# One change in an attention and feed-forward kernel: another weight decode, weight pieces as single transfers, outputs issued from ScalarE's queue

## The chip, the cores and the metric

The kernel runs on one core of one Trainium2 chip. A core has TensorE (PE, matrix products), VectorE (DVE), ScalarE (ACT), GpSimd (POOL) and SyncE (SP, which here only issues DMA transfers); each engine takes its own list of instructions strictly in order and waits on semaphores for the others. The metric is the device time of one execution in microseconds (us), lower is better. Times of single instructions come from one profiled execution.

## The reference

Sliding-window attention followed by a feed-forward layer, both over 4 batches of 768 tokens:

```python
# q, k, v: [4, 8, 768, 64] float32; n_global = 8, n_local = 96
rel = pos[:, None] - pos[None, :]
is_global = pos[None, :] < n_global
is_local = (rel >= 0) & (rel < n_local)
dist = where(is_global & ~is_local, n_local, abs(rel))
scores = q @ k.T / 8 - slopes[h] * dist          # slopes[h] = 2 ** -(h + 1)
scores = where(is_global | is_local, scores, -1e9)
a = exp(scores - max(scores)); a = a / (sum(a) + 1e-9)
x = (a @ v), heads side by side                  # [3072, 512]
h = x @ w_in                                     # w_in [512, 2048]
g = 0.5 * h * (1 + erf(h / sqrt(2)))
return g @ w_out                                 # w_out [2048, 512]
```

w_in and w_out arrive as float64, 16 MB together. The chip gets them as 64-bit words and has to make float32 of them itself.

## The kernel before

**Products.** Every float32 operand of a large product is kept as a high part in TensorE's fast 32-bit format (fp32r) and a low part, which is the remainder; one product is then three matmuls (high by high, low by high, high by low). `hi_pool` (L145) makes a high part on POOL, `lo_dve` (L148) a remainder on DVE.

**Steps.** The 3,072 tokens are 12 chunks of 256, and the 2,048 columns of the hidden layer are 8 slices of 256. A step T is one chunk with one slice, 96 in all. In a step, `m1` (L468) makes the hidden values h with 24 matmuls; `gelu` applies GELU on ACT (tile gr, L478), takes the high part gh on POOL (L145) and the remainder gl on DVE (L148); `m2` (L495) adds the step to the chunk's result acc with 12 matmuls. At a chunk's last slice ACT copies acc into a tile o (L501), and o goes out by a DMA that SP issues (L502). Attention of a later chunk is woven between (scores s L339 and L343, minimum mn L348 on DVE, exponential L363 on ACT, transposes t L389, probabilities pt L392 and L396, products av L417 and L431). Chunks 0 and 1 (`NATIVE`) do their attention in plain float32 at the start, scaled by xs L422 and turned by xt, xh, xl L452, L454.

**Weights.** The weights are used by all chunks, so they are decoded once, slice by slice at the steps given by `DECODE` (steps −4 to 2, before and around the first products). A slice is four pieces of 128 partitions by 512 words: two of w_in, two of w_out, 32 pieces in all. `load_words` (DMA at L159, issued by SP) brings a piece into a raw buffer, 8 bytes a word as two int32 halves, lw (low) and hw (high); the raw buffers are five of pool `ws`, and four of `stg` for the last slice. A w_in piece is two runs of 2 KB per partition, a w_out piece one of 4 KB. `split_weights` then makes float32 from a piece:

- ACT L184: the rounding bits, lw scaled by 2^-29, as an integer, into lw's place
- DVE L186: high word masked and shifted left by 3, into a tile wb (pool `sm`, tag o, two buffers)
- POOL L188: wb plus the rounding bits, an integer add
- DVE L189: sign and top bit of hw (and) joined with wb (or), into hw's place; this is the weight as float32
- ACT L198: high part winh or wouth (for pieces 12 and 26 POOL does it, `HI_POOL`)
- DVE L200: the remainder winl or woutl (for piece 7 POOL does it, `LO_POOL`)

The decode is right for words within a range of exponents. `check_words` (L209 to L211, three ACT passes on a second load of each piece, at steps 17 to 48, with a scratch tile cq) finds whether one is outside; then a slow general path runs behind the fast one. It does not run with these inputs.

**Order.** A scheduler that simulates the engines sets the order of each engine's list from the program's order and its own costs; waits are placed by data dependence, and by buffers that must come free.

Of the kernel before, what the change touches and what calls it, by code (L numbers as in the profile page):

```python
# [65 lines left out]
class Fast:  # L66
    def __init__(self, tc, ctx, qT, kT, v, w_in, w_out, out, limits):
        self.tc, self.nc = tc, tc.nc
        self.qT, self.kT, self.v, self.w_in, self.w_out, self.out = qT, kT, v, w_in, w_out, out
# [80 lines left out]
    def word_src(self, s, i):  # L150
        if i < 2:
            return self.w_in[i * 256:(i + 1) * 256, s * 512:(s + 1) * 512].rearrange("(d p) f -> p d f", p=P)
        r = s * 256 + (i - 2) * P
        return self.w_out[r:r + P, :].rearrange("p (d f) -> p d f", d=2)

    def load_words(self, s, i, use):
        pool, tag = (self.ws, "ws") if use == "w" and s < NST - 1 else (self.stg, "stage")
        w = pool.tile([P, 2, 256, 2], I32, name=f"{use}{s}_{i}", tag=tag)
        ins = self.nc.sync.dma_start(w.rearrange("p d f t -> p d (f t)"), self.word_src(s, i)).ins  # L159
# [10 lines left out]
    def split_weights(self, s):  # L170
# [9 lines left out]
        for i in range(4):  # L180
            w = self.raw.pop((s, i, "w"))
            lw, hw = w[:, :, :, 0], w[:, :, :, 1]
            a, t = hw, lw
            nc.scalar.activation(out=t, in_=lw.bitcast(U32), func=AF.Copy, scale=2.0 ** -29)  # L184
            bt = self.sm.tile([P, 2, 256], I32, name=f"wb{s}_{i}", tag="o")
            nc.vector.tensor_scalar(out=bt, in0=hw, scalar1=0x07FFFFFF, scalar2=3,  # L186
                                    op0=ALU.bitwise_and, op1=ALU.logical_shift_left)
            nc.gpsimd.tensor_tensor(out=bt, in0=bt, in1=t, op=ALU.add)  # L188
            nc.vector.scalar_tensor_tensor(out=a, in0=hw, scalar=-0x40000000, in1=bt,  # L189
                                           op0=ALU.bitwise_and, op1=ALU.bitwise_or)  # L190
            if i < 2:
                hi, lo = (x[:, 2 * i:2 * i + 2, :] for x in self.win[s])
            else:
                hi, lo = (x[:, i - 2, :].rearrange("p (d f) -> p d f", d=2) for x in self.wout[s])
            if s * 4 + i in HI_POOL:
                self.hi_pool(hi, a.bitcast(F32))
            else:
                nc.scalar.copy(hi, a.bitcast(F32))  # L198
            eng = nc.gpsimd if s * 4 + i in LO_POOL else nc.vector
            eng.tensor_tensor(out=lo, in0=a.bitcast(F32), in1=hi.bitcast(F32), op=ALU.subtract)  # L200
# [282 lines left out]
    def m2(self, t, k):  # L483
# [14 lines left out]
        if s == NST - 1:  # L498
            o = self.sm.tile([P, DM], F32, name=f"o{c}_{k}", tag="o")
            r = c * CT + k * P  # L500
            nc.scalar.copy(o, acc)  # L501
            nc.sync.dma_start(self.out[r:r + P, :], o)  # L502
# [99 lines left out]
def round_words(nc, pool, out, src):  # L602
    n = out.shape[1]
# [3 lines left out]
    nc.sync.dma_start(w.rearrange("p f t -> p (f t)"), src)  # L607
# [31 lines left out]
def general(tc, qT, kT, v, w_in, w_out, out, limits):  # L639
# [131 lines left out]
```

## Time and profile before

| | before |
|---|---|
| time, median of 3 runs | 737.29 us (737.2 to 737.31) |
| span of the profiled execution, the only time of its own that the page gives | 735.9 us |
| TensorE (PE) busy | 709.4 us (96%) |
| VectorE (DVE) busy | 481.6 us (65%) |
| ScalarE (ACT) busy | 420.9 us (57%) |
| GpSimd (POOL) busy | 349.4 us (47%) |
| chain of work that ended last | PE 85%, DVE 8%, DMA 2% |

Busy shares are averages over a span whose parts differ, so the table is read with the one by stretches of time in the prediction: the weights are loaded and decoded in the first 126 us, and from there on the steps run alike. The runs' time is 1.4 us longer than the span of the profiled execution. In the rows below, out<-in gives the tiles, "wb<-wb,w" for example the tile wb made from wb and w; "x32 | 31.3, 978" is the count, the busy time in us and the mean in ns; what stands behind the second bar is idle time of that engine just before, and who ended it.

### The profile page before, as it was taken

Reading aid. Unit: us, or ns where it says so; the run is one execution under the profiler, and the core shown is the slowest. Engines: PE = TensorE matmul, PEld = TensorE weight load, DVE = VectorE, ACT = ScalarE, POOL = GpSimd, SP = SyncE. Lnnn points to the kernel's source line nnn. Section 1 sums busy time; section 2 is a strip of 40 time slices with the busy share of each in tenths; the row PEclk is TensorE's granted clock in tenths of the full one; section 3 lists DMA queues with packets and bytes.
Section 4 is the critical chain, followed back from the end, with each engine's and each line's share of the span. In section 5 each row is a group of like instructions: output and inputs, shape, how many; then the busy total and the mean of one; then the engine's idle time right before and its main releaser. Section 6 shows DMA issues by size and latency. Waiting matters only on the chain.

```text
span 735.9 us, 13621 instructions
## 1 busy us (share of the span) xinstructions
PE 709.4 (96%) x4617; PEld 642.8 (87%) x4617; DVE 481.6 (65%) x1219; ACT 420.9 (57%) x1032; POOL 349.4 (47%) x607
## 2 busy tenths in 40 slices
PE   6899878999999999999999999999999999999996
PEld 4778667899999999999999999999999999999995
DVE  6989999757846856746756757757657758643111
ACT  5658544555759769769669556355355455452101
POOL 4666666674445555543444545543444545431110
PEclk9999999999999999999999999999999999999999
DMA  8964563333526546535546513223213211100000
GB/s 264 263 191 143 175 213 81 117 83 101 146 78 171 166 123 177 158 108 158 160 125 174 153 44 87 72 62 94 76 47 109 83 29 44 45 15 1 29 1 33
DMA packets 78492, 80.92 MB, mean 110 GB/s; under 512 B 12368, under 2 KB 63056, under 8 KB 78416
## 3 DMA queue, kind: packets, MB, share of 16 engines
q1 hardware_dynamic: 78416, 79.98, 37.5%
q8 instruction: 38, 0.62, 0.4%
q14 instruction: 38, 0.31, 0.1%
HBM read 73.66 MB, written 6.29 MB: 109 GB/s over the span
## 4 chain that ended last, share of the span: by engine, by line
PE 85%; DVE 8%; DMA 2%; issue 1%; ACT 1%; SPq 1%; POOL 1%; POOLq 0%; DVEq 0%; ACTq 0%
PE h L468 35%; PE acc L495 33%; PE t L389 5%; PE s L343 5%; PE av L431 5%; DMA w<-w_in 2%; DVE winl L200 2%; DVE w L189 2%; PE s L339 2%; DVE woutl L200 1%; DVE wb L186 1%; PE av L417 1%; DVE gl L148 1%; ACT n L363 0%; DVE n L348 0%
## 5 line engine op out<-in xcount | busy, mean ns | idle before, releaser
L468 PE MATMUL h<-xh,winh 128*128 128x256 f32 x768 | 221.1, 289 | 1.5 <-ACT xh L454 1.4
L468 PE MATMUL h<-xh,winl 128*128 128x256 f32 x768 | 218.6, 285 | 0.4 <-DVE winl L200 0.4
L468 PE MATMUL h<-xl,winh 128*128 128x256 f32 x768 | 218.9, 285 | 0.0
L495 PE MATMUL acc<-wouth,gl 128*128 128x512 f32 x384 | 150.0, 399 | 7.2 <-DVE gl L148 7.2
L495 PE MATMUL acc<-wouth,gh 128*128 128x512 f32 x384 | 154.4, 402 | 0.9 <-POOL gh L145 0.9
L468 PEld LDWEIGHTS h<-xh,winh 128*128 128x128 f32 x768 | 146.9, 192 | 7.2 <-ACT xh L454 1.8
L495 PE MATMUL acc<-woutl,gh 128*128 128x512 f32 x384 | 152.4, 397 | 0.0
L468 PEld LDWEIGHTS h<-xl,winh 128*128 128x128 f32 x768 | 147.2, 192 | 3.7 <-issue 0.3
L148 DVE TENSOR_TENSOR gl<-gr,gh 128x512 fp32r<-128x512 f32 x96 | 68.2, 710 | 122.9 <-POOL gh L145 122.3
L468 PEld LDWEIGHTS h<-xh,winl 128*128 128x128 f32 x768 | 147.3, 192 | 0.8 <-DVE winl L200 0.6
L478 ACT ACTIVATE gr<-h 128x512 f32<-128x512 f32 x96 | 57.3, 597 | 82.9 <-PE h L468 75.0
L376 POOL TENSOR_SCALAR n<-n,su 128x256 f32<-128x256 f32 (+1 forms) x160 | 71.2, 466 | 55.2 <-DVE su L368 37.5
L145 POOL TENSOR_SCALAR gh<-gr 128x512 fp32r<-128x512 f32 x96 | 64.0, 667 | 69.6 <-ACT gr L478 69.6
L363 ACT ACTIVATE n<-n,mn 128x256 f32<-128x256 f32 (+1 forms) x192 | 91.8, 480 | 8.3 <-DVE mn L348 8.0
L145 POOL TENSOR_SCALAR vt<-vr 128x256 fp32r<-128x256 f32 (+1 forms) x80 | 34.1, 426 | 130.8 <-PE av L431 83.6
L495 PEld LDWEIGHTS acc<-wouth,gl 128*128 128x128 f32 x384 | 72.8, 190 | 24.4 <-DVE gl L148 9.0
L495 PEld LDWEIGHTS acc<-wouth,gh 128*128 128x128 f32 x384 | 73.2, 191 | 12.3 <-POOL gh L145 1.3
L495 PEld LDWEIGHTS acc<-woutl,gh 128*128 128x128 f32 x384 | 73.2, 190 | 11.8
L348 DVE CUSTOM_DVE_ANT_0 n<-s,pen 128x256 f32<-128x256 f32 (+1 forms) x192 | 69.3, 394 | 16.1 <-PE s L343 13.6
L396 ACT CAST pt<-t 128x512 fp32r<-128x512 f32 (+1 forms) x80 | 44.3, 553 | 60.6 <-PE t L389 56.2
L438 ACT COPY t<-av 64x256 f32<-64x256 f32 x80 | 29.3, 367 | 83.0 <-PE av L431 79.9
L188 POOL TENSOR_TENSOR wb<-wb,w 128x512 int32<-128x512 int32 x32 | 48.0, 1501 | 36.6 <-DVE wb L186 17.3
(92 smaller groups left out, 1158.2 us busy)
## 6 DMA issues: line engine op xcount, KB each, us to landing
kr<-kT SPq DMA_DIRECT2D x112, 112.0 KB, 2.8
qr<-qT SPq DMA_DIRECT2D x88, 128.0 KB, 2.9
w<-w_in SPq DMA_DIRECT2D x16, 512.0 KB, 4.7
w<-w_out SPq DMA_DIRECT2D x16, 512.0 KB, 4.5
c<-w_in SPq DMA_DIRECT2D x16, 512.0 KB, 4.2
c<-w_out SPq DMA_DIRECT2D x16, 512.0 KB, 4.4
vr<-v SPq DMA_DIRECT2D x48, 128.0 KB, 2.3
out<-o SPq DMA_DIRECT2D x24, 256.0 KB, 2.1
```

Of the source, the lines that this page charges most:

```text
L145: self.nc.gpsimd.tensor_scalar(out=out, in0=in_, scalar1=scale, scalar2=0.0, op0=ALU.mult, op1=ALU.add)
L148: self.nc.vector.tensor_tensor(out=out, in0=in_, in1=hi.bitcast(F32), op=ALU.subtract)
L188: nc.gpsimd.tensor_tensor(out=bt, in0=bt, in1=t, op=ALU.add)
L343: nc.tensor.matmul(sp[:, j, :w], lhsT=qq[:, hh, j * P:(j + 1) * P], rhs=kt[:, t, 0 if first else j, :w], start=t == 0, stop=t == 1)
L348: nc.vector.tensor_tensor_reduce(out=nn[:, j, :w], in0=sp[:, j, :w], in1=pen, scale=-slope(h), scalar=3e38, op0=ALU.add, op1=ALU.min, accu ...
L363: ins = nc.scalar.activation(out=nn[:, j, :w], in_=nn[:, j, :w], func=AF.Exp, bias=mn[:, i:i + 1], scale=-1.0, accum_out=su[:, i:i + 1])
L376: nc.gpsimd.tensor_scalar(out=nn[:, j, :w], in0=nn[:, j, :w], scalar1=su[:, i:i + 1], scalar2=0.0, op0=ALU.mult, op1=ALU.add)
L389: nc.tensor.transpose(tp[:, i, :], nn[:, j, a * P:(a + 1) * P], self.ident)
L396: nc.scalar.copy(pt[:, :, 0, :], tp[:, :n, :])
L468: nc.tensor.matmul(hp[:, f, :], lhsT=w[:, d, f * P:(f + 1) * P], rhs=x[:, d, :], start=n == 0, stop=n == 3 * NP - 1)
L478: self.table(nc.scalar.activation(out=gr, in_=hp, func=AF.Gelu))
L495: nc.tensor.matmul(acc, lhsT=g[:, f, ks], rhs=w[:, f, :], start=s == 0 and n == 0, stop=s == NST - 1 and n == 5)
```

## The change

The host lays both weight arrays out as one array `w` of 32 pieces, each [128, 512] words, so that any piece is one run of 4 KB per partition. The decode becomes:

- ACT L181: the rounding bits as before, but written as a 16-bit integer into the low half of lw
- ACT L182, new: the sign of the high word (−1, 0 or 1) as bfloat16 into the upper half of lw
- DVE L184: high word shifted left by 3, without a mask, into wb
- DVE L185: wb plus lw as an integer add. The sign and rounding bits come in with the one add. The instruction list shows it as a custom instruction (ISA) on 1,024 half-words
- ACT L191: high part, 2 times wb, for all 32 pieces
- DVE L192: the remainder, 2 times wb minus the high part, for all 32 pieces

POOL has no part in the decode any more. The raw buffer is last read by the add; wb is held until the remainder is made. The check works in place on the raw words, with other constants, without the scratch tile. The output DMAs are issued by ACT (L495) behind its copy of acc (L494) instead of by SP.

```diff
-# work that GpSimd takes over from the other engines: weight halves (high, low part), V of a chunk
-HI_POOL, LO_POOL, V_POOL = (12, 26), (7,), (2,)
+V_POOL = (2,)
...
     def load_words(self, s, i, use):
         pool, tag = (self.ws, "ws") if use == "w" and s < NST - 1 else (self.stg, "stage")
-        w = pool.tile([P, 2, 256, 2], I32, name=f"{use}{s}_{i}", tag=tag)
-        ins = self.nc.sync.dma_start(w.rearrange("p d f t -> p d (f t)"), self.word_src(s, i)).ins
+        w = pool.tile([P, 512, 2], I32, name=f"{use}{s}_{i}", tag=tag)
+        ins = self.nc.sync.dma_start(w.rearrange("p f t -> p (f t)"), self.w[s * 4 + i]).ins
...
             w = self.raw.pop((s, i, "w"))
-            lw, hw = w[:, :, :, 0], w[:, :, :, 1]
-            a, t = hw, lw
-            nc.scalar.activation(out=t, in_=lw.bitcast(U32), func=AF.Copy, scale=2.0 ** -29)
-            bt = self.sm.tile([P, 2, 256], I32, name=f"wb{s}_{i}", tag="o")
-            nc.vector.tensor_scalar(out=bt, in0=hw, scalar1=0x07FFFFFF, scalar2=3,
-                                    op0=ALU.bitwise_and, op1=ALU.logical_shift_left)
-            nc.gpsimd.tensor_tensor(out=bt, in0=bt, in1=t, op=ALU.add)
-            nc.vector.scalar_tensor_tensor(out=a, in0=hw, scalar=-0x40000000, in1=bt,
-                                           op0=ALU.bitwise_and, op1=ALU.bitwise_or)
+            lw, hw = w[:, :, 0], w[:, :, 1]
+            half = w.bitcast(U16)
+            nc.scalar.activation(out=half[:, :, 0], in_=lw.bitcast(U32), func=AF.Copy, scale=2.0 ** -29)
+            nc.scalar.activation(out=half[:, :, 1].bitcast(BF16), in_=hw, func=AF.Sign)
+            a = self.sm.tile([P, 512], I32, name=f"wb{s}_{i}", tag="o")
+            nc.vector.tensor_scalar(out=a, in0=hw, scalar1=3, scalar2=None, op0=ALU.logical_shift_left)
+            nc.vector.tensor_tensor(out=a, in0=a, in1=lw, op=ALU.add)
+            af = a.bitcast(F32)
...
-            if s * 4 + i in HI_POOL:
-                self.hi_pool(hi, a.bitcast(F32))
-            else:
-                nc.scalar.copy(hi, a.bitcast(F32))
-            eng = nc.gpsimd if s * 4 + i in LO_POOL else nc.vector
-            eng.tensor_tensor(out=lo, in0=a.bitcast(F32), in1=hi.bitcast(F32), op=ALU.subtract)
+            nc.scalar.activation(out=hi, in_=af, func=AF.Copy, scale=2.0)
+            nc.vector.scalar_tensor_tensor(out=lo, in0=af, scalar=2.0, in1=hi.bitcast(F32),
+                                           op0=ALU.mult, op1=ALU.subtract)
...
-        q = self.stg.tile([P, 2, 256], F32, name=f"cq{n}", tag="stage", padded_shape=[P, 4, 256])
-        nc.scalar.activation(out=q, in_=w[:, :, :, 1], func=AF.Square, scale=2.0 ** -27)
+        q = w[:, :, 1].bitcast(F32)
+        nc.scalar.activation(out=q, in_=w[:, :, 1], func=AF.Square, scale=2.0 ** -27, bias=self.cbias[:, 2:3])
...
             nc.scalar.copy(o, acc)
-            nc.sync.dma_start(self.out[r:r + P, :], o)
+            nc.scalar.dma_start(self.out[r:r + P, :], o)
```

**How the order changes.** In the names below, w4_1 is the raw buffer of slice 4, piece 1, wb4_1 its scratch tile, winh4 and winl4 (wouth4, woutl4) the parts of slice 4; the last number only tells tiles of the program apart. First DVE's list before, around the decode of slice 4:

```order
L148 TENSOR_TENSOR gl1_873<-gr1_874,gh1_872 128x512
L186 TENSOR_SCALAR wb4_2_827<-w4_2_245 128x512
L189 SCALAR_TENSOR_TENSOR w4_1_243<-w4_1_243,wb4_1_820 128x512
L200 TENSOR_TENSOR winl4_809<-w4_0_241,winh4_808 128x512
L186 TENSOR_SCALAR wb4_3_834<-w4_3_247 128x512
L200 TENSOR_TENSOR winl4_809<-w4_1_243,winh4_808 128x512
L189 SCALAR_TENSOR_TENSOR w4_2_245<-w4_2_245,wb4_2_827 128x512
L148 TENSOR_TENSOR xl1_603<-xt1_2_897,xh1_602 128x256
L422 TENSOR_TENSOR xs1_3_913<-av1_3_892,su1_3_665 128x2x2x64
L186 TENSOR_SCALAR wb5_0_972<-w5_0_249 128x512
```

and after, at the same place:

```order
L149 TENSOR_TENSOR gl0_781<-gr0_782,gh0_780 128x512
L184 TENSOR_SCALAR wb4_1_822<-w4_1_244 128x512
L185 ISA wb4_1_822<-w4_1_244,wb4_1_822 128x1024
L192 SCALAR_TENSOR_TENSOR winl4_810<-wb4_0_815,winh4_809 128x512
L184 TENSOR_SCALAR wb4_2_829<-w4_2_246 128x512
L149 TENSOR_TENSOR gl1_874<-gr1_875,gh1_873 128x512
L185 ISA wb4_2_829<-w4_2_246,wb4_2_829 128x1024
L192 SCALAR_TENSOR_TENSOR winl4_810<-wb4_1_822,winh4_809 128x512
L415 TENSOR_TENSOR xs1_2_807<-av1_2_793,su1_2_589 128x2x2x64
L149 TENSOR_TENSOR xl1_604<-xt1_1_798,xh1_603 128x256
```

The place of the and/or (L189) is taken by the add (L185, the ISA row), which stands right behind its own shift (L184) or one instruction after it; before, the POOL add lay between them. The remainder (L192) reads wb and no longer the raw buffer.

ACT's list before, at that place:

```order
L478 ACTIVATE gr1_874<-h1_840 128x512
L184 ACTIVATE w4_1_243<-w4_1_243 128x512
L198 CAST wouth3_717<-w3_3_239 128x512
L184 ACTIVATE w4_2_245<-w4_2_245 128x512
L392 COPY pt1_7_883<-t1_7_878 128x512
L198 CAST winh4_808<-w4_0_241 128x512
L184 ACTIVATE w4_3_247<-w4_3_247 128x512
L198 CAST winh4_808<-w4_1_243 128x512
L478 ACTIVATE gr2_942<-h2_915 128x512
```

and after:

```order
L182 ACTIVATE w4_2_246<-w4_2_246 128x512
L181 ACTIVATE w4_3_248<-w4_3_248 128x512
L385 COPY pt1_5_791<-t1_5_786 128x512
L181 ACTIVATE w5_0_250<-w5_0_250 128x512
L191 ACTIVATE winh4_809<-wb4_0_815 128x512
L471 ACTIVATE gr1_875<-h1_841 128x512
L182 ACTIVATE w4_3_248<-w4_3_248 128x512
L181 ACTIVATE w5_1_252<-w5_1_252 128x512
L191 ACTIVATE winh4_809<-wb4_1_822 128x512
L182 ACTIVATE w5_0_250<-w5_0_250 128x512
```

Three passes per piece stand there (L181, L182, L191) where two stood (L184, L198), and the two that prepare a piece are up to a GELU (L471) apart, because the scheduler puts other work between.

POOL's integer adds (L188) are gone from its list; the high parts gh of GELU stay there (L145 before, L146 after). At the end of the first chunk the outputs stood on SP between loads of the next chunks:

```order
L246 DMA kr3_2_1855<-kT 64x2x256 x2
L502 DMA out<-o0_0_1428 128x512
L252 DMA qr3_0_1573<-qT 64x2x256
L502 DMA out<-o0_1_1470 128x512
L252 DMA qr3_0_1573<-qT 64x2x256
L296 DMA vr2_2_1584<-v 128x2x128
L297 DMA vr2_2_1584<-v 96x2x128
```

and after they stand on ACT, right behind their copies:

```order
L471 ACTIVATE gr8_1419<-h8_1392 128x512
L494 COPY o0_0_1429<-acc0_0_886 128x512
L495 DMA out<-o0_0_1429 128x512
L494 COPY o0_1_1471<-acc0_1_903 128x512
L495 DMA out<-o0_1_1471 128x512
L389 CAST pt2_0_1492<-t2_0_1487 128x4x128
```

Both outputs have moved to ACT's list, ahead of the probabilities pt that follow there; the loads on SP have closed up. PE's list keeps its products in almost the same order, and ACT has as many table loads as before.

More of the change, by code (lines that the diff above doesn't have):

```diff
@@ L12 @@
 U32 = mybir.dt.uint32
+U16 = mybir.dt.uint16
 AF = mybir.ActivationFunctionType
@@ L66, with __init__ @@
 class Fast:
-    def __init__(self, tc, ctx, qT, kT, v, w_in, w_out, out, limits):
+    def __init__(self, tc, ctx, qT, kT, v, w, out, limits):
         self.tc, self.nc = tc, tc.nc
-        self.qT, self.kT, self.v, self.w_in, self.w_out, self.out = qT, kT, v, w_in, w_out, out
+        self.qT, self.kT, self.v, self.w, self.out = qT, kT, v, w, out
         self.limits = limits
@@ L112, in consts @@
         self.wbad = const.tile([P, 32], F32, name="wbad")
-        self.cbias = const.tile([P, 2], F32, name="cbias")
-        nc.vector.memset(self.cbias[:, 0:1], -65.0)
-        nc.vector.memset(self.cbias[:, 1:2], -240.0)
+        self.cbias = const.tile([P, 3], F32, name="cbias")
+        for i, x in enumerate((-64.25, -63.0, 0.5)):
+            nc.vector.memset(self.cbias[:, i:i + 1], x)
         ta = self.stg.tile([P, 4, 256], F32, name="ta", tag="stage")
@@ L602, in round_words @@
 def round_words(nc, pool, out, src):
-    n = out.shape[1]
+    n = 512
     ti = lambda name: pool.tile([P, n], I32, name=name)
@@ L606, in round_words @@
     w = pool.tile([P, n, 2], I32, name="r_w")
-    nc.sync.dma_start(w.rearrange("p f t -> p (f t)"), src)
+    for k, x in enumerate(src):
+        m = n // len(src)
+        nc.sync.dma_start(w[:, k * m:(k + 1) * m, :].rearrange("p f t -> p (f t)"), x)
     lw, hw = w[:, :, 0], w[:, :, 1]
@@ L636, in round_words, with general @@
     nc.vector.tensor_copy(out, m)
-def general(tc, qT, kT, v, w_in, w_out, out, limits):
+def general(tc, qT, kT, v, w, out, limits):
     nc = tc.nc
@@ L654, in general @@
                 for f in range(NP):
+                    cols = slice(d % 2 * 512, d % 2 * 512 + 512)
                     round_words(nc, rw, wi[:, d, f * 512:(f + 1) * 512],
-                                w_in[d * P:(d + 1) * P, f * 1024:(f + 1) * 1024])
+                                [w[(2 * f + k) * 4 + d // 2, :, cols] for k in range(2)])
             for f in range(NF):
-                round_words(nc, rw, wo[:, f, :], w_out[f * P:(f + 1) * P, :])
+                round_words(nc, rw, wo[:, f, :], [w[f // 2 * 4 + 2 + f % 2]])
         icol = cst.tile([P, S], I32, name="g_icol")
@@ L734, in general, with body @@
                 nc.sync.dma_start(out[bass.ds(b * S + i * P, P), :], o)
-def body(tc, qT, kT, v, w_in, w_out, limits, out):
+def body(tc, qT, kT, v, w, limits, out):
     nc = tc.nc
-    w_in, w_out = w_in.bitcast(I32), w_out.bitcast(I32)
+    w = w.bitcast(I32)
     with tc.tile_pool(name="flagp", bufs=1) as fp:
@@ L742, in body @@
         with ExitStack() as ctx:
-            fast = Fast(tc, ctx, qT, kT, v, w_in, w_out, out, limits)
+            fast = Fast(tc, ctx, qT, kT, v, w, out, limits)
             fast.run()
@@ L747, in body @@
         with tc.If(fv):
-            general(tc, qT, kT, v, w_in, w_out, out, limits)
+            general(tc, qT, kT, v, w, out, limits)
 def kernel(q, k, v, n_global, n_local, moe_w_in, moe_w_out):
@@ L760 @@
         "v": np.ascontiguousarray(v.transpose(0, 2, 1, 3)).reshape(B, S, DM),
-        "w_in": np.ascontiguousarray(moe_w_in).view(np.int64),
-        "w_out": np.ascontiguousarray(moe_w_out).view(np.int64),
+        "w": np.ascontiguousarray(w),
         "limits": np.array([n_local, n_global]),
```

12 lines of the change are left out of this document (5 added, 7 removed).

## The prediction

> **What bounds the kernel now.** I read three views in this order: a table of busy time by stretch of the span, the list of what TensorE (PE) waits for, and the groups of VectorE (DVE), GpSimd (POOL) and ScalarE (ACT) work in the one stretch where PE has holes. The columns of the first are PE, weight load, DVE, ACT and POOL busy time, each with its count, then the clock that PE was granted, the DMA share and the traffic.
>
> ```profile
> core 0: us, PE busy (x) PEld busy (x) DVE busy (x) ACT busy (x) POOL busy (x), PEclk, DMA share, GB/s
> 12.00:37.00 25.00, 21.83 (x83) 17.95 (x84) 22.68 (x53) 17.10 (x45) 16.31 (x14) 1.00 0.97 288
> 37.00:60.00 23.00, 23.00 (x106) 18.19 (x106) 20.52 (x53) 14.54 (x40) 15.48 (x17) 1.00 0.59 173
> 60.00:126.00 66.00, 54.55 (x333) 46.78 (x332) 65.71 (x100) 34.79 (x67) 40.48 (x33) 0.95 0.50 156
> 126.00:200.00 74.00, 73.52 (x506) 67.79 (x505) 54.03 (x151) 44.50 (x113) 43.98 (x86) 1.00 0.38 108
> 200.00:400.00 200.00, 200.00 (x1361) 184.86 (x1360) 130.35 (x353) 155.57 (x377) 95.64 (x186) 1.00 0.52 147
> ```
>
> From 126 us on PE is full (73.52 of 74, then 200 of 200), and the change leaves its matmuls alone: whatever happens to another engine there is worth nothing unless it makes PE wait. From 60 to 126 PE has 66.00 − 54.55 = 11.45 us of holes while DVE is busy 65.71 of 66.00: DVE bounds this stretch. From 12 to 37 there are 3.17 us of holes under a DMA share of 0.97, and from 37 to 60 there are none. So 14.6 us is the most that filling holes behind 12 us can bring.
>
> Who is waited for in the stretch from 60 to 126, and the only wait after it:
>
> ```profile
> PE acc L495 <- DVE gl L148: 7.2, 5, 2.3
> PE xt L452 <- DVE xs L422: 2.0, 1, 2.0
> ...
> PE s L343 <- DVE k L148: 0.4, 1, 0.4
> ```
>
> The reader is to see that the decode itself is hardly waited for. It is the GELU remainder gl that comes late, since it stands in the DVE's line behind decode work.
>
> **VectorE's side of the change.** The DVE and POOL groups of the same stretch (busy us, mean ns of one):
>
> ```profile
> L189 DVE SCALAR_TENSOR_TENSOR w<-w,wb 128x512 int32<-128x512 int32 x20 | 19.8, 990 | 0.0
> L200 DVE TENSOR_TENSOR winl<-w,winh 128x512 fp32r<-128x512 f32 x10 | 14.5, 1452 | 0.0
> L200 DVE TENSOR_TENSOR woutl<-w,wouth 128x512 fp32r<-128x512 f32 x12 | 14.2, 1181 | 0.1
> L186 DVE TENSOR_SCALAR wb<-w 128x512 int32<-128x512 int32 x19 | 10.4, 550 | 0.1
> L188 POOL TENSOR_TENSOR wb<-wb,w 128x512 int32<-128x512 int32 x20 | 30.9, 1547 | 21.2 <-DVE wb L186 16.1 <-ACT winh L198 2.0 <-ACT xh L454 1.7
> ```
>
> and a few of them one by one (start, duration):
>
> ```profile
> 84.89 0.68 DVE L189 SCALAR_TENSOR_TENSOR w<-w,wb 128x512 int32<-128x512 int32 x1
> ...
> 88.15 0.68 DVE L200 TENSOR_TENSOR woutl<-w,wouth 128x512 fp32r<-128x512 f32 x1
> 88.75 1.79 DVE L189 SCALAR_TENSOR_TENSOR w<-w,wb 128x512 int32<-128x512 int32 x1
> 90.80 0.41 DVE L186 TENSOR_SCALAR wb<-w 128x512 int32<-128x512 int32 x1
> ...
> 93.47 0.84 DVE L186 TENSOR_SCALAR wb<-w 128x512 int32<-128x512 int32 x1
> ...
> 88.46 1.53 POOL L188 TENSOR_TENSOR wb<-wb,w 128x512 int32<-128x512 int32 x1 [1.72 <-ACT xh L454]
> 92.97 1.06 POOL L145 TENSOR_SCALAR gh<-gr 128x512 fp32r<-128x512 f32 x1
> ```
>
> The same DVE instruction takes 0.68 us alone and 1.79 us when POOL's integer add L188 (88.46 to 89.99) lies over it: 1.11 us of its life is the POOL add's. So the means are inflated, and the excess over 0.68 is what the adds cost DVE: L189 20 × (0.990 − 0.682) = 6.2, winl 10 × (1.452 − 0.682) = 7.7, woutl 12 × (1.181 − 0.682) = 6.0, together 19.9 us. I leave out L186's excess, 19 × 0.14 = 2.7, since the row at 93.47 shows it beside POOL's gh, which stays. Taking L188 off POOL gives −19.9 us of DVE time in this stretch (at most −22.6).
>
> The and/or L189 goes and one integer add comes in its place. In the changed kernel's instruction order it is a custom instruction on 1,024 half-words, and the trace has no 16-bit DVE instruction. From below it is bounded by L189 itself, 0.68: same words, two inputs, one of them every second word. From above by a custom instruction that handles one element per step:
>
> ```profile
> L348 DVE CUSTOM_DVE_ANT_0 n<-s,pen 128x256 f32<-128x256 f32 x24 | 9.3, 415 | 1.3 <-PE s L339 1.3
> L348 DVE CUSTOM_DVE_ANT_0 n<-s,pen 128x128 f32<-128x128 f32 x4 | 1.1, 269 | 0.0
> ```
>
> 128 more elements cost 146 ns, so 1,024 would take 0.415 + 768 × 0.00114 = 1.29 us. I take 0.80, near L189, because the bytes per partition are L189's and L348 shows no surcharge for being custom (the plain 0.41 us of a 256-element row). That is +0.12 × 20 = +2.4 us (0 to +12.2). The shift loses its mask and stays at 0.41. The remainder becomes a three-operand form of the same 512 elements; L189 and L200 are such a pair, both 0.68, so nothing. One remainder comes back from POOL, +0.6, put here at worst. Net on DVE between 60 and 126: −19.9 + 2.4 + 0.6 = −17 us, 65.7 to about 49, which is less than PE's 54.55. DVE stops being the bound; PE or ACT is next.
>
> **ScalarE's side.** All 32 pieces get one more ACT pass (the sign), and the two high halves that POOL made come to ACT. Nearest rows, first one by one, then the groups from 12 to 126 us with the idle time before them:
>
> ```profile
> 15.87 0.70 ACT L184 ACTIVATE w<-w 128x512 int32<-128x512 uint32 x1
> 16.44 0.67 ACT L198 CAST winh<-w 128x512 fp32r<-128x512 f32 x1
> L184 ACT ACTIVATE w<-w 128x512 int32<-128x512 uint32 x32 | 21.9, 686 | 12.5 <-DMA w<-w_in 6.9 <-DMA w<-w_out 5.6
> L198 ACT CAST wouth<-w 128x512 fp32r<-128x512 f32 x15 | 10.0, 668 | 11.4 <-DVE w L189 11.3
> ```
>
> Starts are 0.57 apart, so a pass occupies ACT for 0.57 (0.70 if nothing overlaps). From 60 to 126 that is 20 × 0.57 + 2 × 0.57 = +12.5 us: 34.8 becomes 47. ACT is the engine to watch. The most that it is busy over a long stretch in this trace is 155.57 of 200 (0.78); at 0.78 its 47 us need 60 us, at PE's floor of 54.55 it would have to be busy 0.87 of the time. Its old idle time was partly waiting for the very DVE instructions that shrink (L198 for L189, 11.3 us). I take the middle of the two, 57 us for the stretch of 66: −9. From 12 to 37 the loads are at 0.97, so of the 3.17 us there I take 1, for POOL being freer. ACT's table loads stay the same in number.
>
> **Loads, outputs, checks.** A piece as one contiguous run:
>
> ```profile
> w<-w_in SPq DMA_DIRECT2D x16, 512.0 KB, 4.7
> w<-w_out SPq DMA_DIRECT2D x16, 512.0 KB, 4.5
> SPq L159 <- DVE winl L200: 17.0, 6, 4.3
> SPq L502 <- ACT o L501: 112.2, 17, 39.7
> L502 SPq DMA_DIRECT2D out<-o x24: 337/368/867, 134.3 to 730.5; - x24
> ```
>
> w_out pieces already have that form, so 0.2 us of latency for each of 16 pieces, hidden because loads wait for free buffers (17.0 us for winl alone); if that cover went, 3 us. The raw buffer now comes free after the add, two instructions earlier, which can only help; the wb buffer (two of them) is instead held until the remainder is done, but the next shift stands behind that remainder on the same engine anyway: 0. The outputs leave SP, where loads stood 112.2 us behind them, yet PE lost 0.4 us after 126: nothing to gain. On ACT's queue they cost 24 × 0.37 = 9 us over 600, behind which GELU and exponentials stand; ACT is at 0.78 at worst (200 to 400) and PE never waits for it there: 0, and 9 us if ACT were full. At the end it shows:
>
> ```profile
> 729.64 1.60 SPq L502 DMA_DIRECT2D out<-o  x2
> 729.93 0.58 ACT L501 COPY o<-acc 128x512 f32<-128x512 f32 x1 [0.32 <-PE acc L495]
> ```
>
> The last copy must now wait for the first output's issue on its own engine; with 0.37 to 0.87 from 729.64 it starts 0.1 to 0.6 late: +0.3. The check keeps its three ACT passes and loses a scratch tile: 0, hidden like the outputs.
>
> **Sum.** −9 − 1 + 0.3 = −9.7. The profiled execution has a span of 735.9 us; the runs give 737.2 to 737.31, median 737.29, so 1.4 us lies around the span, and I keep it. 735.9 − 9.7 + 1.4 = 727.6 us, 722 to 732 for this case: 722 with all 14.6 us of holes gone, 732 with ACT at 0.78 and the add dearer than taken. A measurement of this kernel can tell about 0.2% (1.5 us) from no change.
>
> **Rivals.**
> (a) The add goes at one half-word per step, 1.29 us. DVE between 60 and 126 is then 65.7 − 19.9 + 12.2 + 0.6 = 58.6, above PE's and level with ACT's need; two engines in order that feed each other do not both run full, so I give 62 of 66: about 733. For it speaks that one operand is every second word; against it that L189 reads so too, at 0.68. The Trainium skill (VectorE: DVE Perf Modes, "Mode 2×_1P — pack two bf16 into one 32-bit read") says that two 16-bit elements a cycle need a 16-bit type and step ±1, which adjacent halves within a word meet and every second word does not: by that rule this rival holds, 733 in place of 727.6. No row here has a 16-bit instruction that could test it.
>
> (b) Slower. ACT takes DVE's place: rounding, sign and high half of every piece, GELU and the PSUM copies now stand in one fixed line, DVE's add waits for the sign, its remainder for the high half, and gl behind them. The 47 us of ACT fill 66 at a busy share of 0.71; below that the stretch gets longer. From 12 to 37 ACT is at 17.10 of 25 (0.68), which would give 69, +3; at 0.64 it is 73, +7. I price it at +5: 742. Against it: it waited then for loads (12.5 us) and for DVE (11.3), not for itself.
>
> (c) The clock comes too. Two rows inside the stretch:
>
> ```profile
> 80.00:90.00 10.00, 7.69 (x40) 6.24 (x39) 10.00 (x13) 4.56 (x9) 6.39 (x5) 0.83 0.56 183
> 100.00:110.00 10.00, 6.96 (x36) 5.83 (x35) 9.96 (x12) 6.08 (x12) 6.56 (x6) 0.83 0.73 261
> ```
>
> PE got 0.83 of its clock there, 2 × 10 × 0.17 = 3.4 us lost. With denser work PE's floor falls from 54.55 to 51.2, and if ACT follows to 53 the stretch gives −13, with −1 before it: 723, 720 at best. The Trainium skill (TensorE: Matmul & The Clock Gate, "Part 1: The HAM clock gate") says that the clock halves after an idle window of about 3.4 us; the longest wait listed here is 2.3 us, so the trace shows the loss but not plainly that cause.
>
> (d) No change: the stretch is paced by something else than DVE's length, the loads, say. Against it: the DMA share is 0.50 at 156 GB/s, where 12 to 37 moved 288. About 737.
>
> **Chances.** Main case 0.54, (a) 0.16, (b) 0.09, (c) 0.15, (d) 0.06. (b) is the slower side, 0.09; (d) is same, 0.06; the rest faster, 0.85. The range leaves out (b), (d) and the far end of (c): 719 to 735. The time is that of the main case.
>
> **What would show it.** L189 and L188 gone; the remainder at 0.68 with no 1.79 rows; the add's duration between 0.68 and 1.29 (near 0.80); DVE busy about 49 us of work where 65.7 stood, ACT about 47; PE's wait for gl well under 7.2 us; PE full from about 116 us on instead of 126. Wrong if ACT shows as what PE or DVE waits for with the stretch as long as before, if the sign takes much more than 0.70 us, or if holes open in PE after the stretch, around the outputs on ACT.

## The result, and the profile after

The changed kernel takes 797.15 us (median of 4, 794.09 to 799.18) against 737.25 before, a ratio of 1.081 (1.078 to 1.084): 60 us slower, where 727.6 was forecast. The rival for a slower outcome said 742. All runs named below are compared with runs of the kernel before on the same chip. Two executions in which PE was slow throughout are left out of the times, e8 (1,375 us, of which only durations of single instructions are read) and one of the twelve of e18 (1,115 us).

The table by stretch of the profiled execution after (columns as in the prediction's first table; its span is 793.7 us):

```profile
12.00:37.00 25.00, 16.10 (x57) 12.07 (x57) 14.43 (x45) 23.75 (x44) 3.22 (x5) 1.00 1.00 284
37.00:60.00 23.00, 21.94 (x74) 16.88 (x73) 18.35 (x48) 23.00 (x36) 7.14 (x12) 1.00 0.70 197
60.00:126.00 66.00, 55.02 (x316) 48.64 (x316) 38.29 (x89) 61.49 (x93) 5.10 (x8) 0.92 0.41 132
126.00:200.00 74.00, 68.32 (x440) 61.79 (x438) 47.19 (x116) 41.93 (x94) 34.03 (x63) 0.96 0.33 93
200.00:400.00 200.00, 179.15 (x1158) 157.82 (x1157) 117.48 (x314) 138.80 (x328) 80.95 (x161) 1.00 0.45 128
400.00:700.00 300.00, 293.90 (x1991) 269.69 (x1991) 190.97 (x519) 161.77 (x414) 140.99 (x277) 1.00 0.28 80
```

Two things are new. Up to 126 us ACT is the full engine (23.75 of 25, 23.00 of 23, 61.49 of 66), with DVE down from 65.71 to 38.29; PE starts fewer matmuls from 12 to 126 us (57 + 74 + 316 against 83 + 106 + 333). And from 200 to 400, where PE had been full, it has 20.85 us of holes, with no engine full. The time was lost in two places, and the second was not in the forecast at all.

ACT's groups of the decode, 60 to 126 us:

```profile
L181 ACT ACTIVATE w<-w 128x512 uint16<-128x512 uint32 x17 | 23.3, 1371 | 2.3 <-DMA w<-w 2.3
L182 ACT ACTIVATE w<-w 128x512 bf16<-128x512 int32 x16 | 21.6, 1351 | 0.2
L191 ACT ACTIVATE winh<-wb 128x512 fp32r<-128x512 f32 x8 | 5.2, 658 | 0.0
```

The high part takes 0.66 us as before; the two passes that write 16-bit halves take 1.37 and 1.35, where the like pass had taken 0.686.

The DVE groups of the same stretch are as the forecast had them, the add included:

```profile
L185 DVE CUSTOM_DVE_ANT_0 wb<-w,wb 128x1024 uint16<-128x1024 uint16 x16 | 11.5, 729 | 0.2
L192 DVE SCALAR_TENSOR_TENSOR winl<-wb,winh 128x512 fp32r<-128x512 f32 x8 | 5.4, 690 | 6.9 <-ACT winh L191 6.8
```

The second place shows in the check's first pass, before and after (all 32, idle time of ACT just before them behind the second bar):

```profile
L209 ACT ACTIVATE cq<-c 128x512 f32<-128x512 int32 x32 | 21.5, 672 | 4.1 <-DVE k L148 2.3 <-DMA c<-w_in 1.6
```

```profile
L202 ACT ACTIVATE c<-c,cbias 128x512 f32<-128x512 int32 x32 | 24.1, 762 | 68.8 <-DMA c<-w 61.9 <-DVE gl L149 6.4 <-issue 0.3
```

and at one place in SP's and ACT's timelines after (the load of c is issued at 252.73, behind the loads of q that SP had in front):

```profile
251.42 1.26 SPq L245 DMA_DIRECT2D qr<-qT  x2
252.73 0.59 SPq L154 DMA_DIRECT2D c<-w  x1
```

```profile
250.18 0.48 ACT L389 CAST pt<-t 128x384 fp32r<-128x384 f32 x1
256.70 0.77 ACT L202 ACTIVATE c<-c,cbias 128x512 f32<-128x512 int32 x1 [6.04 <-DMA c<-w]
259.98 0.60 ACT L471 ACTIVATE gr<-h 128x512 f32<-128x512 f32 x1
```

SP had stood still until 247.19, when the third pass of the check before (L204) gave its buffer free. ACT stands idle for 6.04 us in front of a check that nobody waits for, and behind it in the fixed line stand PSUM copies (L431) and a GELU, on which PE's work hangs. 61.9 us of ACT's time goes that way. What PE itself waits for between 126 and 450 us, where it had waited 0.4 us in all before (the four longest):

```profile
PE av L424 <- DVE pt L149: 9.6, 10, 1.8
PE h L461 <- ACT gr L471: 4.1, 3, 2.1
PE acc L488 <- POOL gh L146: 3.5, 8, 0.7
PE s L336 <- DVE mn L341: 3.5, 2, 1.9
```

The pt of the first row is made from a copy of ACT's (L389), the gh of the third from ACT's GELU. The check loads themselves stand in the chain of work that ended last, with 8% of the span, and PE's share of it is 46% where it was 85%:

```profile
PE 46%; ACT 28%; DMA 11%; DVE 7%; issue 4%; SPq 2%; POOL 1%; ACTq 0%; DVEq 0%; POOLq 0%
PE h L461 20%; PE acc L488 19%; DMA c<-w 8%; ACT n L356 5%; ACT w L181 5%; ACT w L182 4%; PE av L424 3%; PE s L336 2%; PE t L382 2%; ACT c L203 2%; ACT c L204 2%; DMA w<-w 2%; ACT gr L471 2%; ACT L471 2%; ACT c L202 2%
```

### The profile page after: what moved, and what is told of

Read it like the earlier page. It is cut to its first block, busy times and chain, and to the rows that moved or that the text cites. A ratio compares the mean times of both kernels' runs of the same rounds, so it can differ in the third digit from the quotient of the medians.

```text
span 793.7 us, 13516 instructions
## 1 busy us (share of the span) xinstructions
PE 728.9 (92%) x4617; PEld 650.4 (82%) x4617; DVE 456.2 (57%) x1221; ACT 477.8 (60%) x1066; POOL 290.8 (37%) x572
## 4 chain that ended last, share of the span: by engine, by line
PE 46%; ACT 28%; DMA 11%; DVE 7%; issue 4%; SPq 2%; POOL 1%; ACTq 0%; DVEq 0%; POOLq 0%
PE h L461 20%; PE acc L488 19%; DMA c<-w 8%; ACT n L356 5%; ACT w L181 5%; ACT w L182 4%; PE av L424 3%; PE s L336 2%; PE t L382 2%; ACT c L203 2%; ACT c L204 2%; DMA w<-w 2%; ACT gr L471 2%; ACT L471 2%; ACT c L202 2%
## 5 line engine op out<-in xcount | busy, mean ns | idle before, releaser
L461 PE MATMUL h<-xh,winh 128*128 128x256 f32 x768 | 224.6, 293 | 18.1 <-ACT gr L471 9.3
L461 PE MATMUL h<-xl,winh 128*128 128x256 f32 x768 | 221.6, 289 | 0.0
L461 PE MATMUL h<-xh,winl 128*128 128x256 f32 x768 | 220.9, 288 | 0.0
L461 PEld LDWEIGHTS h<-xh,winh 128*128 128x128 f32 x768 | 149.4, 195 | 24.9 <-ACT gr L471 10.4
L461 PEld LDWEIGHTS h<-xl,winh 128*128 128x128 f32 x768 | 150.0, 195 | 4.7 <-issue 0.7
L461 PEld LDWEIGHTS h<-xh,winl 128*128 128x128 f32 x768 | 149.9, 195 | 1.6 <-DVE wb L184 0.7
L149 DVE TENSOR_TENSOR gl<-gr,gh 128x512 fp32r<-128x512 f32 x96 | 71.2, 742 | 127.6 <-POOL gh L146 127.4
L146 POOL TENSOR_SCALAR gh<-gr 128x512 fp32r<-128x512 f32 x96 | 62.0, 645 | 168.3 <-ACT gr L471 168.0
L471 ACT ACTIVATE gr<-h 128x512 f32<-128x512 f32 x96 | 57.7, 601 | 89.3 <-PE h L461 76.7
L146 POOL TENSOR_SCALAR vt<-vr 128x256 fp32r<-128x256 f32 (+1 forms) x80 | 32.6, 407 | 132.7 <-PE av L424 57.8
L389 ACT CAST pt<-t 128x512 fp32r<-128x512 f32 (+1 forms) x80 | 44.3, 555 | 53.4 <-PE t L382 52.0
L432 DVE TENSOR_TENSOR t<-av,t 64x256 f32<-64x256 f32 x80 | 33.6, 420 | 55.9 <-ACT t L431 55.0
L382 PE MATMUL t<-ident,n 128*128 128x128 f32 x352 | 59.4, 290 | 6.8 <-POOL n L369 2.7
```

Source lines behind the costliest of these rows:

```text
L146: self.nc.gpsimd.tensor_scalar(out=out, in0=in_, scalar1=scale, scalar2=0.0, op0=ALU.mult, op1=ALU.add)
L149: self.nc.vector.tensor_tensor(out=out, in0=in_, in1=hi.bitcast(F32), op=ALU.subtract)
L382: nc.tensor.transpose(tp[:, i, :], nn[:, j, a * P:(a + 1) * P], self.ident)
L389: nc.scalar.copy(pt[:, :, 0, :], tp[:, :n, :])
L432: nc.vector.tensor_tensor(out=t1[hr], in0=av[hr, :, 1, :], in1=t1[hr], op=ALU.add)
L461: nc.tensor.matmul(hp[:, f, :], lhsT=w[:, d, f * P:(f + 1) * P], rhs=x[:, d, :], start=n == 0, stop=n == 3 * NP - 1)
```

## The experiments

Edits are against the changed kernel unless another is named.

**Whose part is it?** Four kernels, each with one part undone.

e1_old_check, the scratch tile of the check back:

```diff
-        q = w[:, :, 1].bitcast(F32)
+        q = self.stg.tile([P, 512], F32, name=f"cq{n}", tag="stage", padded_shape=[P, 1024])
```

> The changed kernel with one thing undone: the check's first pass writes a scratch tile again, so a check's raw words are free after one ScalarE pass and not after three. In the changed kernel ScalarE waits 61.9 us for check loads (c <- w), and PE has 31 us of holes between 140 and 450 us. Theory CHECK (the in-place check keeps the staging buffer, so the next load and with it ScalarE's fixed line come late): those waits fall to the 2 us or so of the kernel before, the 40 us lost behind 142 us come back, time 750 to 762. Theory OUTPUTS (the output DMAs' move to ScalarE's queue upsets the order of loads): no change, 792 to 800. Theory LATE START (the decode ends late and everything behind only follows): no change either, 792 to 800, and the waits for check loads stay.

Measured: 753.61 us (753.21 to 754.5), 43.5 us less. From 200 to 400 PE is full again:

```profile
200.00:400.00 200.00, 200.00 (x1365) 184.91 (x1364) 132.90 (x357) 155.38 (x368) 97.32 (x196) 1.00 0.50 144
```

e2_out_sp, the outputs back on SP:

```diff
-            nc.scalar.dma_start(self.out[r:r + P, :], o)
+            nc.sync.dma_start(self.out[r:r + P, :], o)
```

> The changed kernel with one thing undone: the outputs are issued from SP's queue again. Theory OUTPUTS: time falls by about 40 us to 750 to 765 and ScalarE's waits for check loads go. Theory CHECK: within 5 us of the changed kernel, 790 to 802, the waits for check loads (62 us) stay.

Measured: 794.12 us (792.52 to 794.56). ACT's waits for check loads stay (55.2 us), so the outputs' queue is not the cause.

e3_old_decode, the decode of before in the new layout:

> The changed kernel with the decode of before (rounding bits by ScalarE in full words, shift, add on GpSimd, and/or, high and low part; pieces 7, 12 and 26 as before); single transfers, in-place check and outputs on ScalarE's queue stay. Theory DECODE PLUS CHECK (16 us lost in the decode by 142 us, 42 us behind it by the check): 775 to 785. Theory LATE START (all of the loss comes from the decode): 735 to 745. If the check alone is the whole loss: 792 to 800.

Measured: 772.8 us (770.88 to 773.76), 24 us less and a little below the 775 expected, with the check's waits still there (50.4 us). Theory LATE START falls: the check costs its part whenever the decode ends.

e4_wide, whole words instead of halves:

```diff
-            nc.scalar.activation(out=half[:, :, 0], in_=lw.bitcast(U32), func=AF.Copy, scale=2.0 ** -29)
-            nc.scalar.activation(out=half[:, :, 1].bitcast(BF16), in_=hw, func=AF.Sign)
+            nc.scalar.activation(out=lw, in_=lw.bitcast(U32), func=AF.Copy, scale=2.0 ** -29)
+            nc.scalar.activation(out=lw.bitcast(F32), in_=hw, func=AF.Sign)
```

> The changed kernel with the two ScalarE passes of the decode writing whole 32-bit words over the low word (rounding bits as int32, then the sign as float32 over it) in place of 16-bit halves of it; the number of instructions, inputs and functions are the same, but the rounding bits are lost, so the decoded weights are not the reference's. Theory HALF-WORD WRITES (the 1.36 us of L181 and L182, where the like pass took 0.69, come from writing 16-bit elements): both passes 0.56 to 0.70 us, ScalarE busy 45 to 50 us less before 142 us, and the decode stretch ends 15 to 25 us earlier: time 772 to 782 with the check's loss still in it. Theory STRIDED READ OR SIGN (the cost lies in the read or the function): passes stay at 1.3 to 1.4 us, time 792 to 800.

Measured: 769.74 us (767.1 to 772.76), 27.4 us less, a little more than expected. The two passes (min, median and max in ns):

```profile
L181 ACT ACTIVATE w<-w x32: 657/678/706, 13.1 to 106.1; 128x512 int32<-128x512 uint32 x32
L182 ACT ACTIVATE w<-w x32: 655/678/729, 14.0 to 106.8; 128x512 f32<-128x512 int32 x32
```

Neither the function nor the reading of every second word is slow; the 16-bit writing in this form is.

e9_wide_scratch, e1 and e4 together:

> Both causes taken out of the changed kernel at once: whole-word writes in the two ScalarE passes (the rounding bits are lost, so the weights are not the reference's) and the check with its scratch tile. Theory TWO CAUSES (half-word writes 27 us, missing scratch tile 43.5 us, nothing else): 797.2 - 27.4 - 43.5 = 726, between 722 and 731, which is where the forecast put the change. Rival (the two overlap, or the output queue and the single transfers cost something too): 732 to 745.

Measured: 730.9 us (728.95 to 732.82), ratio 0.9906 (0.9874 to 0.9937). With both causes out, the rest of the change takes about 6 us less than the kernel before. The stretch that the forecast worked on:

```profile
60.00:126.00 66.00, 62.02 (x406) 56.64 (x405) 50.43 (x111) 46.34 (x94) 10.45 (x16) 0.94 0.48 153
```

The forecast's terms stand here: DVE 50.43 (about 49 forecast), ACT 46.34 (47), PE's holes 3.98 of 66 where they were 11.45. So the two causes account for the miss, less some 5 us (the single effects add up to 726). In its profile PE is 20.34 of 23 us busy from 37 to 60, at a granted clock of 0.58, where before it was full at 1.00; whether the 5 us lie there, no run tests.

**Why are half-words dear?** e8_forms writes the rounding pass in four ways (the edit shortened to the outputs):

```diff
+            if i == 0:    out=ah[:, 0:512]                        # 16-bit, packed, in the wb tile
+            elif i == 1:  out=ah (f t)->(f t), t=2, [:, :, 0]      # 16-bit, 4 bytes apart, in the wb tile
+            elif i == 2:  out=half[:, :, 0]                        # 16-bit, 8 bytes apart, in lw
+            else:         out=lw                                   # int32, 8 bytes apart, in lw
```

> The changed kernel with the rounding-bit pass written in four ways, one for each piece of a slice: 16-bit side by side into the scratch tile; 16-bit into every second half-word of the scratch tile (4 bytes apart); 16-bit into the low half of lw as in the changed kernel (8 bytes apart); int32 into lw. The first three lose rounding bits for their pieces or leave the raw low word in the add, so the weights are not the reference's; only durations are read. Theory WIDTH (any 16-bit output costs double): 1.36 us three times, 0.68 for int32. Theory PARTIAL WORD (16-bit elements that lie apart cost double, packed ones do not): 0.68, 1.36, 1.36, 0.68. Theory STRIDE (8 bytes apart): 0.68, 0.68, 1.36, 0.68.

```profile
L184 ACT ACTIVATE wb<-w x8: 656/672/707, 12.6 to 142.3; 128x512 uint16<-128x512 uint32 x8
L186 ACT ACTIVATE wb<-w x8: 779/793/848, 14.6 to 144.1; 128x512 uint16<-128x512 uint32 x8
L188 ACT ACTIVATE w<-w x8: 1327/1352/1401, 17.7 to 131.2; 128x512 uint16<-128x512 uint32 x8
L190 ACT ACTIVATE w<-w x8: 637/686/743, 19.4 to 139.1; 128x512 int32<-128x512 uint32 x8
```

A 16-bit write is as fast as a 32-bit one when packed, a little slower at 4 bytes apart, twice as long at 8. But the third form is also the only 16-bit one in place. e26_forms256 (256 elements a pass) tells distance from place: L185 8 bytes apart in another tile, L188 8 bytes apart in place, L191 4 bytes apart in another tile, L194 int32 in place.

> The rounding pass of the changed kernel in two halves of 256 elements, in four ways by piece: 16-bit 8 bytes apart into the scratch tile; 16-bit 8 bytes apart in place in lw; 16-bit 4 bytes apart into the scratch tile; int32 in place. The first and third leave the raw low word in the add, so the weights are not the reference's; only durations are read. From the 512-element rows (0.672 packed, 0.793 at 4 bytes, 1.352 at 8 bytes in place, 0.686 int32 in place) half the length should take about 0.41 for int32. Theory DISTANCE: the first two alike, 0.70 to 0.80 us, the third about 0.47. Theory IN PLACE: only the second at 0.70 to 0.80, the first 0.45 to 0.55.

```profile
L185 ACT ACTIVATE wb<-w x16: 751/816/872, 13.1 to 123.0; 128x256 uint16<-128x256 uint32 x16
L188 ACT ACTIVATE w<-w x16: 752/791/850, 15.8 to 115.2; 128x256 uint16<-128x256 uint32 x16
L191 ACT ACTIVATE wb<-w x16: 462/484/580, 20.8 to 127.9; 128x256 uint16<-128x256 uint32 x16
L194 ACT ACTIVATE w<-w x16: 412/436/525, 19.7 to 120.0; 128x256 int32<-128x256 uint32 x16
```

It is the distance (0.816 and 0.791 alike). The Trainium skill (SBUF — State Buffer, "Door 1: The DMA port swizzle", its note on cachelines) says that a line has 16 bytes, that two hits on a line are enough for full rate, and that bf16 data may therefore be strided by 8 elements for free. By that rule 4 elements (8 bytes) cost nothing. Here ScalarE's output at that distance cost double, 1.352 us as uint16 and 1.351 as bf16 (L182), and int32 at the same distance nothing (0.686), so for these writes the measurement decides against it.

**Why does the check in place cost 43 us?** e11_hold keeps the raw words through all three passes, and the scratch tile too (against e1):

```diff
-        nc.scalar.activation(out=q, in_=q, func=AF.Relu, ...)
+        nc.scalar.activation(out=w[:, :, 1].bitcast(F32), in_=q, func=AF.Relu, ...)
```

> The variant with the scratch tile for the check (753.61 us), but the third pass writes its result into the raw words, so they are held through all three passes as in the changed kernel while the scratch tile is still taken in turn. Theory HOLD (what costs is that the raw words are kept for three passes): the check loads come late again, their lead over the first pass falls from a median of 11.5 us to about 5, time 785 to 800. Theory TURN (what costs is the missing scratch tile, which changes the turn in which the four staging buffers are given out and so the order of loads and check passes): leads stay near 11, time 752 to 760.

Measured: 757.36 us (755.48 to 758.61), the load's lead over the first pass a median of 9.6 us (from the load's issue to the start of the pass; 11.4 in e1, 11.5 before, 5.0 in the changed kernel). Holding the words for three passes is worth at most some 4 us of the 43.5.

e15_dummy takes a scratch tile and lets GpSimd touch it:

```diff
+        nc.gpsimd.memset(self.stg.tile([P, 512], F32, name=f"cq{n}", tag="stage", padded_shape=[P, 1024])[:, 0:1], 0.0)
```

> The changed kernel as it is, check in place, with one thing added: at each check a scratch tile is taken from the four staging buffers and a single column of it is set to zero by GpSimd. It does no work for the result. Theory TURN (the missing scratch tile changes the turn of the staging buffers and so the order of loads and check passes): leads of the check loads back near 11 us, time 752 to 760 as with the real scratch. Theory IN PLACE (three passes over the raw words, with a bias tile, are the cost): 785 to 800.

Measured: 794.23 us (792.62 to 796.43), lead 4.6 us, ACT's wait for check loads 54.7 us. TURN, which e11 had seemed to bear out, is wrong too: giving out one more staging buffer does nothing by itself. So I compared the written orders. In ACT's list the first pass of check n stands behind GELU n+12 or n+13 in the changed kernel and in e15, and behind n+15 to n+17 in e1 and e11: three to four steps later. That the place moves with the scratch tile of the pass is shown (e1 changes nothing else); the reason is my reading: a pass that needs a scratch buffer has to wait for one in the scheduler's reckoning as well. e23_pin adds one rule of order and nothing else:

```diff
-        nc.scalar.activation(out=q, in_=w[:, :, 1], func=AF.Square, ...)
+        first = nc.scalar.activation(out=q, in_=w[:, :, 1], func=AF.Square, ...)
+        self.after(first.ins, self.last_gelu, "check behind its step")
...
+        self.last_gelu = g.ins
```

> The changed kernel as it is, check in place and no scratch tile, with one order added: the first pass of check n must stand behind GELU n+17 in ScalarE's list (it stood behind n+12 or n+13; with the scratch tile behind n+15 to n+17). Theory PLACE (the pass stands in ScalarE's fixed line about four steps ahead of where it did, so the line waits for a load that SP could not issue earlier): leads near 11 us, ScalarE's waits for check loads under 10 us, time 750 to 760. Theory IN PLACE (the passes themselves, or the staging buffers they hold, are the cost): 785 to 800.

Measured: 758.11 us (755.44 to 760.17), the lead a median of 16.6 us. ACT's wait for check loads is gone, and nothing else of the check in place was undone. The first pass as it then stands:

```profile
L202 ACT ACTIVATE c<-c,cbias x32: 740/758/782, 212.8 to 431.6; 128x512 f32<-128x512 int32 x32
...
its engine sat idle before it (us, times) until:
who waited for it (us, times):
```

Place is the cause: 39 of the 43.5 us come back by that one rule of order, with the words held in place through all three passes as in the changed kernel.

**Versions that keep the idea.** e16_pool_sign (against e1) makes the sign on GpSimd:

```diff
+            nc.scalar.activation(out=lw, in_=lw.bitcast(U32), func=AF.Copy, scale=2.0 ** -29)
+            nc.gpsimd.tensor_scalar(out=half[:, :, 1].bitcast(BF16), in0=hw, scalar1=0.0, scalar2=-0.5,
+                                    op0=ALU.is_ge, op1=ALU.add)
...
+            nc.scalar.activation(out=hi, in_=af, func=AF.Copy, scale=4.0)
```

> The variant with the scratch tile for the check (753.61 us) with the sign made on GpSimd (compare with zero, minus one half, as bfloat16 into the upper half of lw; the later scale becomes 4) and the rounding bits written by ScalarE as whole words. ScalarE is back at two passes of 0.68 us a piece, VectorE has three instructions a piece. Theory HALF-WORD WRITES AND CHECK ARE ALL: the decode stretch is then about what was forecast for the change, time 722 to 732, VectorE about 50 us busy between 60 and 126. Rival: GpSimd's single-input pass stretches VectorE's shift (0.41 to 0.84 beside gh before) or takes over 1.5 us by writing half-words, then it becomes the next wait: 735 to 750.

Measured: 757.4 us (754.47 to 758.18). The rival, and worse than it said: GpSimd takes 2.86 us for such a pass and is the full engine itself, busy 23.89 of 25 us from 12 to 37, 22.44 of 23 to 60, and 55.65 of 66 from 60 to 126.

```profile
L182 POOL TENSOR_SCALAR w<-w 128x512 bf16<-128x512 int32 x32 | 89.6, 2857 | 11.4 <-ACT w L181 7.7 <-DVE q L271 2.1 <-DMA qr<-qT 1.6
```

e18_halves_in_wb (against e1) lets ACT write both halves 4 bytes apart into the wb tile:

> The variant with the scratch tile for the check (753.61 us), with the same two 16-bit ScalarE results written 4 bytes apart into the wb tile in place of 8 bytes apart into lw; the shift goes in place into the high words, and the add takes both. All of the change's decode is kept. In the four-forms run a 16-bit pass took 0.79 us at 4 bytes apart and 1.35 at 8. Theory STRIDE: both passes 0.79 us, ScalarE about 50 us busy between 60 and 126, time 726 to 734, faster than the kernel before. Rival (in-place reading and writing, not the distance, or wb being held from the rounding on, which leaves two pieces in flight): 736 to 752.

Measured: passes of 0.78 and 0.77 us. The stride theory holds for the durations. The time is 734.89 to 737.27 us in ten of the eleven executions, above the 734 expected, and 724.65 in the other; what makes that one 10 us shorter stays open. The median of the eleven is 735.78 against 736.8 before, so a gain is not shown. (A ratio of 0.9949, 0.9911 to 0.9988, is that of the five shortest alone.)

e13_dve_sign (against e1) makes the sign by one 16-bit VectorE instruction:

```diff
+            nc.scalar.activation(out=lw, in_=lw.bitcast(U32), func=AF.Copy, scale=2.0 ** -29)
+            nc.vector.tensor_scalar(out=half[:, :, 1], in0=half[:, :, 3], scalar1=0x8000, scalar2=0x3F80,
+                                    op0=ALU.bitwise_and, op1=ALU.bitwise_or)
```

> The variant with the scratch tile for the check (753.61 us), with the sign made on VectorE: one 16-bit and/or of the upper half of the high word into the upper half of lw, and the rounding bits by ScalarE as whole words. Four VectorE instructions a piece and two ScalarE passes. If VectorE writes half-words 8 bytes apart at its usual rate (0.41 to 0.68 us): VectorE 50 + 20 x 0.34 to 0.60, 57 to 62 us between 60 and 126, time 730 to 736. If it pays double like ScalarE (0.8 to 1.4 us): 738 to 752.

Measured: 731.86 us (730.26 to 737.46), ratio 0.9941 (0.9917 to 0.9966); the instruction takes 0.744 us in the median, 512 elements 8 bytes apart.

e25_best, the same with the outputs on SP:

> The variant with the sign on VectorE and the scratch tile for the check (731.86 us), with the outputs issued from SP again. If the outputs on ScalarE's queue cost what the first experiment on them showed (797.15 to 794.12): 728 to 731, faster than the kernel before by 0.7 to 1.2%. If that difference was only that of runs, 731 to 733.

Measured: 731.4 us (726.63 to 737.36), ratio 0.9938 (0.9909 to 0.9968), the best whole version, and no different from e13: the output queue is worth nothing that these runs can tell.

e5_add_dve, the kernel before with its add moved from GpSimd to VectorE and nothing else:

```diff
-            nc.gpsimd.tensor_tensor(out=bt, in0=bt, in1=t, op=ALU.add)
+            nc.vector.tensor_tensor(out=bt, in0=bt, in1=t, op=ALU.add)
```

> The kernel before with one change: the integer add of the decode (L188) on VectorE in place of GpSimd. It measured 0.69 us alone in the changed kernel. From 60 to 126 VectorE loses 19.9 us of stretching and gains 20 x 0.60: 65.7 to about 57.7. Theory STRETCH (the GpSimd add costs VectorE 1.11 us each time and this bounds the stretch): 728 to 733. Rival (VectorE only waits elsewhere, the stretch is paced by loads or ScalarE): 736 to 739.

Measured: 736.64 us (732.21 to 737.87), ratio 0.9985 (0.9962 to 1.0008): no change, against my theory. The stretching is gone all the same (12 to 130 us):

```profile
L188 DVE CUSTOM_DVE_ANT_0 wb<-w,wb 128x1024 uint16<-128x1024 uint16 x32 | 24.0, 751 | 0.0
L189 DVE SCALAR_TENSOR_TENSOR w<-w,wb 128x512 int32<-128x512 int32 x32 | 22.4, 701 | 0.0
```

L189 falls from 978 ns to 701. From 60 to 126:

```profile
60.00:126.00 66.00, 57.01 (x374) 50.25 (x373) 60.73 (x123) 37.33 (x71) 13.95 (x14) 1.00 0.51 163
```

DVE is busy 60.73 of 66 there, not 57.7, and PE waits 4.9 us for POOL's gh (12 to 160 us) where it had waited 7.2 for gl. PE does 374 matmuls in this stretch where it had done 333, but only 77 from 37 to 60 where it had done 106, full both times; why was not followed.

## Why the prediction was wrong, point by point

- **What bounds the kernel, and the stretching.** The stretching was read rightly: with the GpSimd add gone no remainder takes 1.79 us (median 692 ns, the longest 1,220), and e5 takes L189 from 978 ns to 701 by moving that add alone. "DVE bounds this stretch" is not borne out with it: e5 takes 5 us off DVE's busy time there and the time stays. That the whole is worth 9 us was too much even with both causes out (e9: 6).
- **The add.** Right: 0.69 in the median, 0.73 in the mean, against 0.80 taken and a range of 0.68 to 1.29. So rival (a) fell, and with it the use that the prediction made there of the Trainium skill's rule: with one operand at every second word, 1,024 half-words took 0.69 us, the time of a plain instruction on 512 elements and about half of the 1.29 that one half-word per step would have taken. The prediction was wrong that the trace before has no 16-bit VectorE instruction: L131, on bf16, takes 0.29 us for 128 elements, no less than L348's 0.27 on float32. Of operands at every second word it says nothing.
- **The ScalarE passes.** The step that failed first. "Starts are 0.57 apart, so a pass occupies ACT for 0.57 (0.70 if nothing overlaps)" was taken from L184, of the same shape but with int32 output. The 16-bit outputs at 8 bytes apart took 1.36, and the rounding pass, which I counted as unchanged, took it too. ACT's added work is 32 × (1.36 − 0.69) + 32 × 1.36 = 65 us by durations, not the 18 us of 32 passes at 0.57; ACT's busy time rose from 420.9 to 477.8 us. That is rival (b)'s mechanism at a price that it did not have: ACT takes DVE's place, 27 us (e4; 23 with the check undone first, e1 to e9). Of the prediction's own signs of being wrong this one, "if the sign takes much more than 0.70 us", came with 1.35.
- **The check.** The larger step that failed: "The check keeps its three ACT passes and loses a scratch tile: 0, hidden like the outputs." I counted its instructions and left out its place. Losing the tile let the scheduler put the first pass three to four steps earlier in ACT's list, ahead of its data: 43.5 us (e1; 39 with the cheap passes, e4 to e9), of which 39 come back by moving it (e23). Holes in PE behind the stretch were named as a sign too, but "around the outputs on ACT", which had no part in them (e2). The changed order was there to be read, against the GELU numbers.
- **Outputs, loads, tail.** The outputs at 0 to 3 us (e2, e25) bear out the 0. At the end the last copy started 0.1 us behind the first output's issue (0.34 us) and 0.18 us after its last matmul, where that had been 0.03: within the +0.3.
- **Clock.** Rival (c)'s resource moved the other way: the granted clock from 60 to 126 is 0.92 where it was 0.95, and the same 4,617 matmuls keep PE busy 728.9 us where they took 709.4. A group of matmuls of h, from 37 to 70 us after and from 52 to 80 before:

```profile
L461 PE MATMUL h<-xl,winh 128*128 128x256 f32 x13 | 5.9, 452 | 0.0
```

```profile
L468 PE MATMUL h<-xl,winh 128*128 128x256 f32 x18 | 5.2, 293 | 0.0
```

Before, too, such matmuls were slow at first (489 ns from 37 to 51 us); after, this slow phase lasts some 20 us longer. The clock column reads 1.00 there in both, so only the durations show this phase, and its cause stays open. Holes in PE are not needed for it: in e8 the like matmuls take 441 ns in the mean of all 768, with PE busy 99% of the span.

## What to carry to other kernels

Price an instruction by a row with its own output type and distance, not just by shape; a pass that writes 16-bit fields into wider records is another instruction. And when a buffer is taken out, look at what it had held back: an instruction that nobody waits for does harm when the written order puts it ahead of its data on an engine that others wait for.

## What the runs showed of the hardware

- ScalarE, 512 elements: 16-bit output packed 0.672 us, 4 bytes apart 0.793, 8 bytes apart 1.352; int32 at 8 bytes apart 0.686.
- GpSimd, 512 elements, int32 to 16-bit at 8 bytes apart: 2.86 us (e16). VectorE, 16-bit to 16-bit at 8 bytes apart: 0.744.
- The integer add of VectorE on 512 words: 0.69 us, one operand at every second word, the same as a plain two-input instruction of 512 elements.
